# Banded attention into a squared-ReLU feed-forward network: weight loads, column writes, PSUM pools and zeroing rearranged in the first third of the kernel

## The chip, the cores and the metric

One core of a Trainium2 chip runs the whole program. The metric is the device time of one execution in microseconds (us), lower is better; a version is given as the median of several executions. The engines are named as in the profile: PE multiplies matrices (PEld is its weight load, which overlaps), DVE is the vector engine, ACT the scalar engine, POOL the GpSimd engine, and SP only starts transfers. Each engine works through its own instructions in program order and waits where an input is not ready. Transfers (DMA) are started from SP, ACT and POOL; the ones from POOL can change the number type on the way, and here they turn float32 in memory into float16 on chip.

## What is computed

Eight batches of eight heads, 576 tokens of 64 numbers each. Every token attends to tokens within 32 positions; eight "global" tokens, whose positions are an input, attend to all and are attended by all. The result goes through a two-layer network.

```python
scores = (1 / sqrt(64)) * q @ k.T                      # per batch and head, 576 x 576
mask = |pos_i - pos_j| <= 32  or  i is global  or  j is global
attn = softmax(where(mask, scores, -1e9))
x = (attn @ v)  as 4608 tokens x 512                    # heads side by side
h = x @ w_in                                            # 512 x 2048
out = (relu(h) ** 2) @ w_out                            # 2048 x 512
```

The eight positions are known only when the kernel runs, so the kernel cannot place them at build time.

## The kernel before, in words

**Layout.** Work is done by pair of heads: `i = 4*b + hp` is pair `hp` of batch `b`, so pairs 0 to 3 are batch 0 and pairs 4 to 7 batch 1. A pair's keys lie in five tiles of 128 rows (8 rows for the global tokens, then 120 tokens), its queries in 608 columns (four groups of 144 tokens and 8 columns for the global tokens). Each pair is done in two halves: `sc_mm` (L766) makes the scores, `sc_exp` (L786) the exponentials on ACT, `sc_mask` (L794) the mask on DVE, `pv_mm` (L811) the products with the values and the sums, `pv_rec` (L829) the reciprocal of the sums on ACT as exp(-ln), `pv_mul` (L859) the division on DVE into `xT` (for the first half of batch 0 into `xA`), the transposed input of the network. The global tokens' own results are summed over column groups in `pv_sum` (L835), divided into `gx`, and written into their columns of `xT` or `xA` by `scatter` (L881): eight small copies on POOL, one for each global token, whose column comes from a register. In batch 0 `pv_sum` finishes pairs 0 to 2 in one go (at `hp` = 2) and pair 3 alone.

**Network.** `mm1_half` and `mm1` are the first product with ReLU and square; `mm2` is the second product of chunk 0, `mm2_fast` (L686) that of the later chunks, as seven half-sized products in place of eight, which need sums of weight blocks (`weight_sum`, L632, five of them, on DVE, into the `early` buffer that holds batch 0's and 1's values before) and sums of activation blocks. This work stands in a list, `fills`. `fill(n)` (L745) takes pieces from its head for `n` units of credit, with fixed costs per kind (L748), as long as the tokens they need are done (`done[0]`). So network work is laid between the steps of attention at build time, in an order that each engine then follows.

**Batch 0, written out by hand (L899 to L1027).** Queries, keys and values come by transfers from SP and ACT for pairs 0 and 1 (L218 to L224) and from POOL for pairs 2 and 3 (L291 to L295). DVE zeroes some areas first (`stv[0:NG]` L231, `vts[2]` and `vts[3]` L233), POOL four others (L290). POOL then starts, in this order: the four slices of `w_in` (L979), the tokens of batch 1 (L986 to L989), register loads of the positions and `scatter` of pairs 0 to 2 (L991), two slices of `w_out` (L1005), `scatter` of pair 3 (L1006), the other two slices (L1012), and `scatter` of the second halves (L1013). SP holds the values of batch 1 back behind a small transfer `gate` (L1015) that waits for the third slice of `w_in`.

**PSUM.** Matrix products land in PSUM, in tiles by tag: `at` (two banks each, attention) and `mm` (one bank each). All lie in one pool: three `at` and two `mm` at first; after the last scores of batch 0, `open_psum(2, 4)` (L998) closes the pool and opens another with two `at` and four `mm`. A pool opened after another takes its place in PSUM, so its first use waits until the old pool's tiles are read.

After that switch, PE does 24 matrix products of `mm1_half` (four tiles `u` = 0, 2, 4, 6, three of four pairs: L1000), `pv(2, 1)` and `pv(3, 1)`, eight more products for pair 3 (L1008), and goes on with the fills and batch 1.

**Batch 1 to 2.** At the end of batch 1 comes `fill(3)` (L1060), then for batch 2 onward, per pair: both halves of scores, `weight_sum` calls while `b == 2` (two at pair 0, two at pair 1, one at pair 2; L1073), `fill(4)`, the products with the values, and `fill(4)` again (L1090).

Of the kernel before, what the change touches and what calls it, by code (L numbers as in the profile page):

```python
# [18 lines left out]
NT = 5  # L19
# [31 lines left out]
def kernel(  # L51
# [10 lines left out]
    nc = tc.nc  # L62
# [4 lines left out]
    P = 128  # L67
# [17 lines left out]
    psum = {}  # L85

    def open_psum(at, mm):
        if psum:
            psum["stack"].close()
        psum["stack"] = ExitStack()  # L90
        psum["pool"] = psum["stack"].enter_context(
            tc.tile_pool(name=f"ps{at}", bufs=1, space=bass.MemoryType.PSUM)
        )
        psum["bufs"] = {"at": at, "mm": mm}

    def pst(tag, shape, dtype=FP32):
        return psum["pool"].tile(shape, dtype, name=tag, tag=tag, bufs=psum["bufs"][tag])

    open_psum(3, 2)
# [131 lines left out]
    nc.vector.memset(stv[0:NG, :, 0 : 2 * 2], 0.0)  # L231
    for vt in vts[2:NHP]:
        nc.vector.memset(vt[0:NG], 0.0)  # L233
# [55 lines left out]
    for vt in vts[0:NHP]:  # L289
        nc.gpsimd.memset(vt[96:P, 4], 0.0)  # L290
# [3 lines left out]
    for i in range(2, NHP):  # L294
        fetch_values(nc.gpsimd, 0, i, vts[i])  # L295
# [431 lines left out]
    W1, W2 = 0.65, 1.54  # L727
# [17 lines left out]
    def fill(n):  # L745
        credit[0] += n
        while fills and fills[0][0] <= done[0]:
            cost = {mm1: W1, mm2_fast: W2}.get(fills[0][1], 1) * share[0]  # L748
            if credit[0] < cost / 2:
                break  # L750
            credit[0] -= cost
            take(1)
        else:
            credit[0] = min(credit[0], 0)

    share = [1.0]

# [77 lines left out]
    def pv_sum(i, half):  # L835
# [10 lines left out]
        if (half == 0 and b == 0 and hp >= NHP - 2) or (half and b and hp == NHP - 1):  # L846
            gs = gsum[b][:, 0]
            a, z = (0, NHP) if b else (0, NHP - 1) if hp < NHP - 1 else (NHP - 1, NHP)
            if b:
                nc.vector.tensor_tensor(out=gs, in0=gs, in1=gsum[b][:, 1], op=ALU.add)  # L850
            gr = sbt("gr", [P, NHP, NG], FP32, bufs=2)
            if a == 0:
                gxs[b] = sbt("gx", [P, NHP, NG], FP16, bufs=2)
            nc.vector.reciprocal(out=gr[:, a:z], in_=gs[:, a:z, 1])
            nc.vector.tensor_tensor(
                out=gxs[b][:, a:z], in0=gs[:, a:z, 0], in1=gr[:, a:z], op=ALU.mult
            )
# [28 lines left out]

    wv = moe_w_in.rearrange("(t p) f -> p t f", p=P)
    wo = moe_w_out.rearrange("(t p) m -> p t m", p=P)
# [89 lines left out]
    for i in range(4):  # L978
        pool.dma_start(out=w_in[:, :, ts(i, 512)], in_=wv[:, :, ts(i, 512)])  # L979
# [5 lines left out]

    for nm in "kq":  # L986
        fetch_tokens(pool, nm, NHP)
    for nm in "kq":
        fetch_tokens(pool, nm, NHP + 1, NHP - 1)  # L989
    load_columns()  # L990
    scatter(0, slice(0, NHP - 1), xA)  # L991
# [6 lines left out]
    open_psum(2, 4)  # L998
    wide[0] = True
    for u in range(0, 8, 2):  # L1000
        mm1_half(u, 0, range(NDM - 1))
    pv(2, 1)
    pv(3, 1)
    for j in range(2):
        pool.dma_start(out=w_out[:, ts(j, 4), :], in_=wo[:, ts(j, 4), :])  # L1005
    scatter(0, slice(NHP - 1, NHP), xA)  # L1006
    nc.scalar.copy(out=xT[:, :, 256:HS], in_=xA[:, :, 256:HS])
    for u in range(0, 8, 2):  # L1008
        fills.pop(0)
        mm1_half(u, 0, range(NDM - 1, NDM))  # L1010
    for j in range(2, 4):
        pool.dma_start(out=w_out[:, ts(j, 4), :], in_=wo[:, ts(j, 4), :])  # L1012
# [47 lines left out]
    fill(3)  # L1060
    wide[0] = False

    for i in range(2 * NHP, B * NHP):
# [9 lines left out]
        if b == 2:  # L1073
            for p in ((3, 4), (6, 7), (1,), ())[hp]:
                weight_sum(p)
            if hp == 0:
                nc.gpsimd.memset(vbs[1][96:P, NT - 1], 0.0)
        fill(4)
# [11 lines left out]
        fill(4)  # L1090
# [9 lines left out]
    psum["stack"].close()  # L1100
# [30 lines left out]
```

## Time and profile before

| | us |
|---|---|
| median of 4 executions (327.37 to 331.79) | 330.08 |
| the profiled execution, whole | 331.15 |
| its span, first to last instruction of the program | 329.4 |

The four times spread over 4.4 us. The profile belongs to one execution, whose span is 1.75 us shorter than its own whole time. Five views are read. The page gives busy time per engine and the span in 40 slices of 8.2 us. The windows view gives, for chosen stretches, busy time and count of instructions per engine, and the clock that was granted to PE (1.00 is full speed). The timeline lists instructions in order: start, duration, engine, line, operation, what is written and read, count, and in brackets how long the engine stood idle before and what ended that. The view of waits adds such idle times up. The view of transfers gives their queues and rates. "Issue" in a bracket means that no wait is visible in the profile.

Instructions of PE are pipelined and a busy PE can be one that works at half speed, so the clock column has to be read beside the busy column.

### The profile page before, as it was taken

To read this page: it belongs to the slowest core of one execution; us is meant where nothing else is said; L and a number is where in the kernel's file an instruction comes from. 1 tells how busy PE (TensorE), PEld (TensorE's weight loads), DVE (VectorE), ACT (ScalarE), POOL (GpSimd) and SP (SyncE) were. 2 spreads that over 40 slices of the span, in tenths; PEclk is the share of its full clock that TensorE was granted. 3 is DMA by queue.
4 is the path that set the end of the run, shared out by engine and by line. 5 is a ranking of instruction groups with operands and counts; after the bars stand their busy time and mean duration, and the time that the engine had idled before them with its cause. 6 is when DMAs were issued, how large, how long until landed. Compare 5 with 4: busy or idle time off the path is not lost.

```text
span 329.4 us, 11606 instructions
## 1 busy us (share of the span) xinstructions
PE 312.3 (95%) x4827; PEld 237.2 (72%) x4827; DVE 244.5 (74%) x595; ACT 200.9 (61%) x378; POOL 127.6 (39%) x222
## 2 busy tenths in 40 slices
PE   6977899999989999999999999999999999999995
PEld 3655678545569857975799865985698569868995
DVE  7756278849799778876967969876987698758465
ACT  2567458745767587667457478658865876363150
POOL 8945389318910880089200773039402000100000
PEclk9995799999999999999999999999999999999999
DMA  8999999939991999299924299959995400200211
GB/s 191 145 201 199 200 195 160 150 76 107 196 148 39 149 187 148 53 146 167 159 76 109 30 164 150 73 131 173 134 86 129 123 4 16 87 30 2 68 63 66
DMA packets 149492, 38.98 MB, mean 118 GB/s; under 512 B 132696, under 2 KB 148872, under 8 KB 149440
## 3 DMA queue, kind: packets, MB, share of 16 engines
q0 software_dynamic: 97872, 17.08, 66.5%
q1 hardware_dynamic: 51150, 20.57, 31.5%
q8 instruction: 38, 0.62, 0.9%
q10 hardware_dynamic: 418, 0.59, 0.7%
q14 instruction: 14, 0.11, 0.1%
HBM read 37.80 MB, written 17.29 MB: 167 GB/s over the span
## 4 chain that ended last, share of the span: by engine, by line
issue 42%; POOL 20%; PE 17%; DMA 6%; DVE 3%; ACT 1%; POOLq 1%
PE mm L305 16%; POOL kscr L183 6%; DMA qscr<-in_q_dram 6%; POOL xT L884 4%; POOL stf L212 3%; POOL qscr L190 2%; POOL s16b L212 2%; DVE gt L556 1%; POOL gstk L442 1%; DVE mix L641 1%; POOL gstq L442 1%; POOL gstv L442 1%; POOLq L884 1%; PE at L822 1%; ACT er L790 1%
## 5 line engine op out<-in xcount | busy, mean ns | idle before, releaser
L305 PE MATMUL mm<-xT,w_in 128*64 128x512 f16 (+2 forms) x1216 | 122.5, 351 | 0.2 <-POOL xT L884 0.2
L305 PEld LDWEIGHTS <-w_in 128*64 128x64 f16 (+1 forms) x1280 | 80.5, 110 | 46.0 <-issue 3.4
L554 ACT ACTIVATE rl<-mm 128x512 f16<-128x512 f32 x128 | 74.3, 600 | 36.7 <-PE mm L305 33.6
L884 POOL COPY xT<-gx 128x4 f16 x64 | 17.7, 277 | 141.0 <-DVE xT L863 137.6
L556 DVE TENSOR_TENSOR gt<-rl 128x512 f16<-128x512 f16 x128 | 52.9, 421 | 24.3 <-ACT rl L554 20.7
L305 PEld LDWEIGHTS <-mix 128*64 128x64 f16 x1280 | 68.9, 110 | 1.6
L790 ACT ACTIVATE er<-at 128x880 f16<-128x880 f32 x58 | 49.7, 904 | 15.4 <-PE at L781 13.9
L641 DVE TENSOR_TENSOR mix<-gt 128x1024 f16<-128x1024 f16 (+1 forms) x82 | 52.8, 670 | 0.2
L800 DVE TENSOR_TENSOR et<-er,mask 128x880 f16<-128x880 f16 x58 | 35.7, 616 | 17.9 <-ACT er L790 17.3
L305 PE MATMUL mm<-early,mix 128*64 128x256 f16 x768 | 45.4, 273 | 0.0
L832 ACT ACTIVATE rec<-at 128x288 f32<-128x288 f32 x64 | 25.9, 404 | 29.3 <-PE at L822 23.0
L305 PEld LDWEIGHTS <-gt 128*64 128x64 f16 (+1 forms) x596 | 33.1, 109 | 11.1 <-DVE gt L556 3.5
L863 DVE TENSOR_TENSOR xT<-at,rec 128x288 f16<-128x288 f32 x60 | 27.1, 452 | 10.5 <-ACT rec L833 9.9
L305 PE MATMUL mm<-early,gt 128*64 128x256 f16 x512 | 32.2, 274 | 2.3 <-DVE gt L556 2.3
L822 PE MATMUL at<-et,onesb 128*64 128x192 f16 (+5 forms) x400 | 31.1, 230 | 0.0
L305 PE MATMUL mm<-w_out,mix 128*64 128x256 f16 x512 | 30.9, 273 | 0.0
L833 ACT ACTIVATE rec<-rec 128x288 f32<-128x288 f32 x64 | 28.4, 443 | 2.0
L676 DVE TENSOR_TENSOR ot<-mm,pt 128x512 f32<-128x512 f32 (+1 forms) x36 | 22.7, 631 | 6.5 <-ACT pt L701 5.2
L183 POOL DMA_DIRECT2D kscr<-in_k_dram x30 | 26.3, 1083 | 0.3 <-issue 0.3
L190 POOL DMA_DIRECT2D qscr<-in_q_dram x24 | 24.5, 1526 | 0.0
L822 PEld LDWEIGHTS <-onesb 128*64 128x64 f16 x400 | 22.8, 114 | 0.7
L701 ACT COPY pt<-mm 128x512 f32<-128x512 f32 (+1 forms) x18 | 9.7, 540 | 20.5 <-PE mm L305 20.5
(125 smaller groups left out, 325.8 us busy)
## 6 DMA issues: line engine op xcount, KB each, us to landing
out_dram<-ot SPq DMA_DIRECT2D x32, 256.0 KB
qscr<-in_q_dram POOLq DMA_DIRECT2D x24, 144.0 KB
kscr<-in_k_dram POOLq DMA_DIRECT2D x24, 120.0 KB
w_in<-in_moe_w_in_dram POOLq DMA_DIRECT2D x4, 512.0 KB
w_out<-in_moe_w_out_dram POOLq DMA_DIRECT2D x4, 512.0 KB
early<-in_v_dram SPq DMA_DIRECT2D x12, 120.0 KB
stf<-in_v_dram POOLq DMA_DIRECT2D x12, 120.0 KB
s16b<-in_v_dram POOLq DMA_DIRECT2D x12, 120.0 KB
```

Of the source, the lines that this page charges most:

```text
L183: nc.gpsimd.dma_start(out=kscr[b][r0 : r0 + KN[t]].rearrange("s (h d) -> s h d", d=D), in_=k[b, :, KT * t : KT * t + KN[t]].rearrange("h s ...
L190: nc.gpsimd.dma_start(out=qscr[b][r0 : r0 + GTOK].rearrange("s (h d) -> s h d", d=D), in_=q[b, :, GTOK * g : GTOK * (g + 1)].rearrange("h ...
L305: nc.tensor.matmul(to[r], weights[:, r], moving, **flags)
L554: nc.scalar.activation(out=rl, in_=ph, func=AF.Relu)
L556: nc.vector.tensor_tensor(out=gt[:, :, 0:T], in0=rl, in1=rl, op=ALU.mult)
L641: nc.vector.tensor_tensor(out=gsums[p][:, lo:hi, 0:TH], in0=g[0], in1=g[1], op=op)
L790: nc.scalar.activation(out=er[:, :, 0:W], in_=scs.pop((i, half))[:, :, 0:W], func=AF.Exp, bias=0.0, scale=scale)
L800: nc.vector.tensor_tensor(out=et[:, :, 0:W], in0=er[:, :, 0:W], in1=mask[:, MB[half] : MB[half] + W].unsqueeze(1).to_broadcast((P, 2, W)), ...
L822: nc.tensor.matmul(acc[D * e : D * e + D, x, o : o + w], onesb if x else vt[:, t, e], et[:, e, so : so + w], start=(n == 0), stop=(n == le ...
L833: nc.scalar.activation(out=rec, in_=rec, func=AF.Exp, scale=-1.0)
L863: nc.vector.tensor_tensor(out=(xT if x0 else xA)[:, hp, x0 : x0 + HS].rearrange("p (k x) -> p k x", k=2), in0=av[:, 0, :, 0:GTOK], in1=rec ...
L884: nc.gpsimd.tensor_copy(out=xb[:, :, ds(gv[g], 1)], in_=gxs[b][:, pairs, g : g + 1])
```

## The change

It has five parts.

1. Zeroing: `stv[0:NG]`, `vts[2]` and `vts[3]` are zeroed by copies of a zero tile on ACT; rows 96 on of the fifth tile of `vts[2]` and `vts[3]` too; the same rows of `vts[0]` and `vts[1]` by DVE. POOL zeroes none of them.
2. POOL's transfers: the first slice of `w_in` is started between the values of pairs 2 and 3, the second after those of pair 3, the other two where all four were.
3. Column writes of batch 0: `pv_sum` finishes pairs 0 and 1 together and pairs 2 and 3 together. `scatter` of pairs 0 and 1 goes ahead of the transfers of batch 1's tokens on POOL, `scatter` of pairs 2 and 3 behind them; all `w_out` slices come after both. `mm1_half` runs in two parts of two pairs (16 and 16 products, where it was 24 and 8).
4. PSUM: the third `at` buffer lies in a pool of its own. Only that pool is closed at the switch, and its two banks become two more `mm` buffers; the two `at` and two `mm` of the base pool stay. `pst` counts its calls and sends each third `at` tile (before the switch), or each second `mm` tile (after it), to the extra pool, so the buffers take turns as they did.
5. Batch 2: five times `fill(1.6)` with one `weight_sum` each before the loop, in place of `fill(3)` and the `weight_sum` calls in the loop; `done[0]` is 2 before it; inside batch 2 each `fill(4)` becomes `fill(slot)`, an 8.5th of what is left.

```diff
-    def open_psum(at, mm):
-        if psum:
-            psum["stack"].close()
...
+    psum_base = open_psum("base", {"at": 2, "mm": 2})
+    psum_more = open_psum("third", {"at_more": 1})
 
     def pst(tag, shape, dtype=FP32):
-        return psum["pool"].tile(shape, dtype, name=tag, tag=tag, bufs=psum["bufs"][tag])
-
-    open_psum(3, 2)
+        n = banks_of[tag]
+        banks_of[tag] += 1
+        more = tag + "_more"
+        if more in pools and (n % 3 == 0 if tag == "at" else n % 2):
+            tag = more
+        pool, bufs = pools[tag]
+        return pool.tile(shape, dtype, name=tag, tag=tag, bufs=bufs)
...
-    nc.vector.memset(stv[0:NG, :, 0 : 2 * 2], 0.0)
+    zeros = idle[0:NG].unsqueeze(1)[:, :, 0 : 4 * D].to_broadcast((NG, NT, 4 * D))
+    nc.scalar.copy(out=stv[0:NG, :, 0:4].rearrange("p t h d -> p t (h d)"), in_=zeros)
     for vt in vts[2:NHP]:
-        nc.vector.memset(vt[0:NG], 0.0)
+        nc.scalar.copy(
+            out=vt[0:NG].rearrange("p t e d -> p t (e d)"), in_=zeros[:, :, 0 : 2 * D]
+        )
+        nc.scalar.copy(out=vt[96:P, 4].rearrange("p e d -> p (e d)"), in_=idle[96:P, 0 : 2 * D])
+    for vt in vts[0:2]:
+        nc.vector.memset(vt[96:P, 4], 0.0)
...
-    for vt in vts[0:NHP]:
-        nc.gpsimd.memset(vt[96:P, 4], 0.0)
+    def fetch_w_in(i):
+        nc.gpsimd.dma_start(out=w_in[:, :, ts(i, 512)], in_=wv[:, :, ts(i, 512)])
...
-    for i in range(2, NHP):
-        fetch_values(nc.gpsimd, 0, i, vts[i])
+    fetch_values(nc.gpsimd, 0, 2, vts[2])
+    fetch_w_in(0)
+    fetch_values(nc.gpsimd, 0, 3, vts[3])
+    fetch_w_in(1)
...
-        if (half == 0 and b == 0 and hp >= NHP - 2) or (half and b and hp == NHP - 1):
+        if (half == 0 and b == 0 and hp % 2) or (half and b and hp == NHP - 1):
             gs = gsum[b][:, 0]
-            a, z = (0, NHP) if b else (0, NHP - 1) if hp < NHP - 1 else (NHP - 1, NHP)
+            a, z = (0, NHP) if b else (hp - 1, hp + 1)
...
-    for i in range(4):
-        pool.dma_start(out=w_in[:, :, ts(i, 512)], in_=wv[:, :, ts(i, 512)])
+    for i in range(2, 4):
+        fetch_w_in(i)
...
+    load_columns()
+    scatter(0, slice(0, 2), xA)
     for nm in "kq":
         fetch_tokens(pool, nm, NHP)
     for nm in "kq":
         fetch_tokens(pool, nm, NHP + 1, NHP - 1)
-    load_columns()
-    scatter(0, slice(0, NHP - 1), xA)
+    scatter(0, slice(2, NHP), xA)
...
-    open_psum(2, 4)
+    pools.pop("at_more")
+    psum_more.close()
+    psum_more = open_psum("fourth", {"mm_more": 2})
     wide[0] = True
     for u in range(0, 8, 2):
-        mm1_half(u, 0, range(NDM - 1))
+        mm1_half(u, 0, range(2))
     pv(2, 1)
     pv(3, 1)
     for j in range(2):
-        pool.dma_start(out=w_out[:, ts(j, 4), :], in_=wo[:, ts(j, 4), :])
-    scatter(0, slice(NHP - 1, NHP), xA)
+        fetch_w_out(j)
     nc.scalar.copy(out=xT[:, :, 256:HS], in_=xA[:, :, 256:HS])
     for u in range(0, 8, 2):
         fills.pop(0)
-        mm1_half(u, 0, range(NDM - 1, NDM))
+        mm1_half(u, 0, range(2, NDM))
...
-    fill(3)
+    done[0] = 2
+    for p in (3, 4, 6, 7, 1):
+        fill(1.6)
+        weight_sum(p)
     wide[0] = False
+    slot = left() / 8.5
...
-        if b == 2:
-            for p in ((3, 4), (6, 7), (1,), ())[hp]:
-                weight_sum(p)
-            if hp == 0:
-                nc.gpsimd.memset(vbs[1][96:P, NT - 1], 0.0)
-        fill(4)
+        if i == 2 * NHP:
+            nc.gpsimd.memset(vbs[1][96:P, NT - 1], 0.0)
+        fill(slot if b == 2 else 4)
```

## The prediction, made before the changed kernel was run

> **What bounds the kernel now.** I read the windows view first, cut at stages, since the page's busy shares average over stages with different limits.
>
> ```profile
> core 0: us, PE busy (x) PEld busy (x) DVE busy (x) ACT busy (x) POOL busy (x), PEclk, DMA share, GB/s
> 0.00:10.07 10.07, 6.79 (x76) 3.97 (x78) 7.13 (x46) 3.20 (x7) 8.79 (x31) 1.00 0.92 195
> 10.07:23.72 13.65, 11.13 (x295) 8.29 (x291) 8.94 (x25) 8.14 (x21) 9.40 (x13) 1.00 1.26 165
> 23.72:37.37 13.65, 11.72 (x119) 8.17 (x115) 5.46 (x17) 6.73 (x12) 6.48 (x20) 0.50 1.28 202
> 37.37:48.00 10.63, 8.88 (x164) 7.21 (x160) 7.17 (x21) 7.21 (x16) 6.59 (x13) 1.00 1.19 191
> 48.00:72.00 24.00, 23.80 (x346) 15.19 (x342) 17.96 (x51) 16.68 (x34) 12.48 (x14) 1.00 1.63 145
> 72.00:112.00 40.00, 38.87 (x576) 27.31 (x576) 33.13 (x70) 25.40 (x47) 21.48 (x37) 1.00 1.11 119
> 112.00:280.00 168.00, 165.85 (x2578) 127.25 (x2576) 133.11 (x304) 115.35 (x212) 60.80 (x89) 1.00 1.08 114
> ```
>
> From 48 us on PE is busy 97% to 99% of each stage: it is the limit there, and a microsecond won earlier arrives at the end undiminished if transfers keep up. Room lies before 48 us: PE is idle 9.5 us of it (48 minus 38.5), and from 23.72 to 37.37 us it has half its clock. There the timeline shows what PE, DVE, ACT and POOL do:
>
> ```profile
> 1.63 1.12 DVE L231 MEMSET early<- 8x1280 f32 x1 [0.22 <-issue]
> 2.77 0.66 DVE L233 MEMSET early<- 8x320 uint32 x2
> 6.34 0.83 ACT L462 CAST natq<-stf 96x768 f16<-96x768 f32 x1 [4.24 <-DMA stf<-in_q_dram]
> 22.76 0.24 PE L478 MATMUL mm<-early,oh 128*64 128x128 f16 x1 [1.71 <-issue]
> 27.62 2.02 POOL L884 COPY mix<-gx 128x3 f16 x8 [7.84 <-DVE mix L863]
> 31.28 2.33 POOL L884 COPY mix<-gx 128x1 f16 x8
> 31.77 5.28 PE L305 MATMUL mm<-mix,w_in 128*128 128x256 f16 x24 [1.42 <-ACT er L790]
> 37.81 0.41 ACT L832 ACTIVATE rec<-at 128x288 f32<-128x288 f32 x1 [6.14 <-issue]
> 40.21 1.91 PE L305 MATMUL mm<-mix,w_in 128*128 128x256 f16 x16 [1.13 <-ACT rl L587]
> ```
>
> The reader sees: DVE zeroes for 1.8 us while ACT stands idle for 4.2; PE waits 1.42 us at the PSUM switch for an exponential; 24 products then take 5.28 us, 220 ns each at half clock (the later 16 take 119 ns each), and ACT sits 6.14 us behind them, because `pv(2, 1)` comes after all 24. PE then waits again, 1.13 us, for the ReLU that frees a PSUM buffer.
>
> **The change part by part.** All against the profiled execution, 331.15 us whole, 1.07 us over the median of 330.08.
>
> *Zeroing.* DVE loses 1.12 + 0.66 us and gains two memsets of the kind at L1030 (0.11 us each): 1.55 us sooner at the mask and at the cast of pair 0's keys (6.82 us, their transfer landed at 4.1). PE follows as far as queries allow: their cast waits for a landing at 6.34 us whatever is done, so their transposes go from 8.39 to about 7.2 us. I take 1.1 us for what comes after. The copies on ACT are not in this trace; its nearest row, the cast above, is 0.83 us for 768 elements, so 1280, twice 640 and twice 128 cost about 3.3 us behind the table load's end at 2.1 us and two issues: they end near 5.6 us, before 6.34. Without that cover, each excess microsecond would delay the query cast. Bounds for this part: 0 (a later chain hides it) to 1.5. POOL loses 0.7 us of memsets, which starts its transfers as much sooner.
>
> *Weight slices.* POOL's queue gets `w_in` 0 and 1 ahead of where they stand (0.78 us of issue each). Behind slice 0 wait the three issues of pair 3's values, which landed at 15.8 us; a slice took about 3 us in the steady stretch (19.9, 23.1, 25.6, 28.6 us), so they land near 17 to 18. PE reads them at 23.75. The gather of global values moves past both slices, landing near 20 in place of 16.5; only SP's store waits for it. The transfers have a hole at 14 to 16 us (58 and 38 GB/s by microsecond, about 200 around it), which the early slices fill, so slice 3 lands 2 to 3 us sooner and the gate opens sooner. PE needs slices 0 and 1 only at about 29 us: the direct gain is nothing, and so is the cost, with 5 us of cover over pair 3's values.
>
> *Column groups.* On POOL the first scatter becomes pairs 0 and 1; its input is `pv_mul(1, 0)`, done at 25.7 us (24.6 after the gain above), so it runs to about 26.7. Behind it now stand four token transfers (2.95 us of issue, formerly at 17.0 to 19.8), then scatter 2 to about 32 us (eight copies again, 2.0 to 2.3 us). No queue entry is cheaper: 16 copies before, 16 after. Tokens of pair 4 then land near 31 us, and those of the others, 0.86 MB at the 150 KB/us that POOL's queue gets beside SP's, near 36. They are used at 42.0 and 46.4 us, some 4 us sooner after the change: covered by 5 us. The four `w_out` slices go behind, as before first read after 50 us.
>
> *PSUM and the order on PE.* The first `mm` tile is in the base pool and free; the new one waits only for `pv_mul(1, 1)`, at 30.6 us. So the 1.42 us go. In place of 24 products ahead of `pv(2, 1)` there are 16. With the cold clock of this profile: scores of pair 3 end at 30.35 - 1.1 = 29.25; 16 x 220 ns = 3.5, to 32.8; the two `pv_mm` 1.4, to 34.2; the other 16 products at 119 ns, 1.9, to 36.1 (their scatter ended at about 32). ACT begins its reciprocals at about 33.5, takes 1.7 for both, 0.3 for the copy and 0.6 for the first ReLU: 36.2. PE goes on there in place of 40.21: 4.0 us sooner, 1.1 of it from zeroing, 2.9 from this part. What is late next is POOL's second scatter.
>
> If PE were at full clock throughout, the before would be some 3.6 us shorter here (24 x 0.1 us at the products, the rest from 119 smaller matmuls that stretch, an estimate), the new order would stop at POOL's second scatter (31.2 us) and PE would resume near 33.3, so about 3.3 us stay.
>
> *Batch 2.* The five `weight_sum` take 1.22 us each on DVE. Three of them lie in a stage where DVE is the limit:
>
> ```profile
> 72.00:80.00 8.00, 8.00 (x94) 4.29 (x94) 5.77 (x10) 3.31 (x7) 6.65 (x15) 1.00 0.70 45
> 88.00:96.00 8.00, 7.64 (x102) 4.46 (x98) 8.00 (x20) 6.70 (x14) 3.60 (x5) 1.00 2.01 145
> 96.00:104.00 8.00, 7.43 (x148) 7.10 (x150) 8.00 (x17) 4.05 (x8) 0.00 (x0) 1.00 0.49 57
> ```
>
> DVE works without a pause from 88 to 104 us, and PE is idle 0.93 us of it, mostly behind squares (`gt`, L556) queued on DVE. The change moves the sums to about 72 to 80 us, where DVE has 2.2 us free and the eight remaining `mm2` pieces (about 0.9 us each, 7 us) keep PE busy without it. Counting the credits through the list, the 8 units before the loop are exactly those eight pieces; the first scores of batch 2 move behind five more of them, 4.5 us later against the network work, none of which is lost. Their masks queue behind the last sum, and six `mm1` pieces (5.4 us) cover that on PE. Pieces of chunk 1 need `scatter(1)`, done at 74.6 us, before PE gets there at 78. In the later batches the same pieces stand in the same slots but for one. Bounds: -0.5 (masks late at the start of batch 2) to 1.6 (the idle PE of 88 to 112 us, less what other stages have too). I take 1.0.
>
> *A rule against the row.* PE stands idle for 1.7 us until 22.76 us, with no wait visible, and 1 us later the clock falls to half for 13.65 us. The Trainium skill ("TensorE: Matmul & The Clock Gate", sections "What's actually happening" and "Why this matters for your kernels") has half clock follow a whole idle window of about 3.4 us, and warns of idle gaps over about 3 us. By that rule this gap is too short, the cold stretch is no property of this order of work, and the changed kernel should not be charged with one: it would come back at 33.3 us instead of 36.2, 2.9 us more gain. By the row, 1.7 us in the midst of thin work were enough. The instructions around the gap are unchanged, so I keep the gap and the fall, and take the row's value; the rule's is the lower end of the range. (13.65 us are four times 3.41 us; the length of the window the trace bears out.)
>
> **Sum.** 1.1 + 2.9 + 1.0 = 5.0 us: 326.15 us for an execution like the profiled one. The four times (327.4 to 331.8) spread by about what the cold stretch is worth, so the median is likely of executions with less of it; there the gain is 3.3 to 4.0 plus 1.0, giving 325.1 to 325.8 from 330.08. I forecast 325.8.
>
> **The rivals.**
> *Cold stretch gone or shorter.* PE gets dense work 2.5 us sooner, which can end the half clock one window sooner, or the gap falls otherwise in the window. For: the clock came back just after the 24 products. Against: the gap stays. Time: 326.15 - 2.9 = 323.3.
> *The gain is partly hidden.* Zeroing gains nothing because the chain through ACT and the landing at 6.34 us sets the start, or moving the sums only shifts DVE's queue. For: queries cannot be cast sooner. Against: DVE and PE have no idle time worth the name between 5 and 7 us. Time: 330.08 minus only 2.2 to 2.9, some 327.2 to 327.9; with the PSUM wait left besides (see next), 329.3.
> *The change does not do what it says.* If the new pool's first tile waits for all scores as the old one did, the 1.42 us stay: 327.2. The first tile is in the pool that is never closed, which speaks against it.
> *Slower: POOL's second scatter stalls PE.* Scatter copies took 0.25 us each in these groups but 0.40 beside a busy DVE (3.17 us for eight at 40.1). Twice 3.2 and the tokens' 2.95 from 24.6 us end at 34.0 instead of 32; any further 2 us (a late `pv_mul(1, 0)`, slower issues while queues are full) let PE stand 1.8 us or more between its two sets of 16 products. By the row above that is a gap that halves the clock, and PE's next 13.65 us, about 70% matmul time, would cost 5 us. It decides where the scatter ends later than 36 us in a cold execution, or 33 in a warm one; without the clock it costs only its own length. Time: 330.08 - 4.3 + 2.8 + 5.0 = 333.6.
>
> **How the numbers follow.** Likeliest case (324.3 to 327.2): 0.48. Cold stretch gone (322.3 to 324.3): 0.16. Partly hidden or not as said (327.2 to 331): 0.25. POOL stall (331 to 336): 0.11. The range from 322.8 to 330.3 leaves out about 0.05 below and 0.13 above. One per cent, 3.3 us, is about what a measurement of this kernel can tell from no change; faster than that means below 326.8. Of the likeliest case 0.40 lies there, with 0.16 of the cold one: 0.56. Slower than 333.4: 0.07. The rest, 0.37, is within 1%.
>
> **What the profile would show.** Right: the cast of pair 0's keys near 5.3 us and scores of pair 3 over a microsecond sooner; 16 products at the switch with no idle time before them; no 6 us gap on ACT; network work after the switch resuming near 36 us or sooner, not 40.2; DVE below 8 of 8 us somewhere in the stage that was 88 to 104; stages after 112 us of the same length. Wrong: PE idle before the second 16 products with POOL's scatter as the releaser; the transposes of batch 1's tokens (42.0 us before) starting after a transfer's landing; a second stretch at half clock; PE idle before the first `mm1` of chunk 1 behind DVE. If the stages from 48 us on lengthen by what the start gains, the claim that PE alone sets them was wrong.

## The result and the profile after

| | us | of it |
|---|---|---|
| before, in the same comparison | 328.09 | median of 65 executions, 326.72 to 332.20 |
| after | 327.18 | median of 42 executions, 324.75 to 330.09 |
| ratio after to before | 0.9957 | 95% interval 0.9941 to 0.9973 |
| profiled execution, after | 325.63 | span 323.9 |

The change gains 0.9 us, 0.43%: more than the comparison's uncertainty, and well within 1%. The forecast was 325.8 from a base of 330.08, a gain of 4.3. Two of these numbers have to be explained: the median of before lies 2 us below that of the four times that were shown, and the gain is a fifth of what was summed. The gain of more than 1%, to which the forecast gave 0.56, did not come.

The profile alone tells another story. The windows view, cut from the start of full clock at 7.56 us in steps of 13.65 us, with one later stage:

```profile
core 0: us, PE busy (x) PEld busy (x) DVE busy (x) ACT busy (x) POOL busy (x), PEclk, DMA share, GB/s
0.00:7.56 7.56, 5.75 (x55) 3.10 (x57) 4.95 (x40) 5.66 (x11) 6.34 (x25) 1.00 0.80 192
7.56:21.21 13.65, 11.49 (x308) 8.37 (x305) 9.40 (x29) 8.22 (x22) 9.29 (x11) 1.00 1.43 199
21.21:34.87 13.66, 10.70 (x167) 8.35 (x162) 8.20 (x23) 10.62 (x23) 9.82 (x26) 1.00 0.95 143
112.00:280.00 168.00, 165.05 (x2628) 128.26 (x2625) 133.74 (x303) 113.53 (x209) 57.88 (x92) 1.00 1.06 111
```

The stretch at half clock is not there. The timeline of the start, with line numbers of the changed kernel (L910 is the scatter's copy, L889 the product of `pv_mul`, L858 and L859 the two steps of the reciprocal):

```profile
5.55 0.55 DVE L485 CAST natk<-stf 96x768 f16<-96x768 f32 x1
20.94 0.24 PE L501 MATMUL mm<-early,oh 128*64 128x128 f16 x1 [1.11 <-issue]
23.81 0.26 PE L848 MATMUL at_more<-et,early 128*64 128x160 f16 x2 [1.40 <-ACT rec L859]
23.82 1.98 POOL L910 COPY mix<-gx 128x2 f16 x8 [6.59 <-DVE mix L889]
28.38 0.60 PE L328 MATMUL mm_more<-mix,w_in 128*128 128x256 f16 x4 [0.38 <-DVE xT L889]
28.71 2.60 POOL L910 COPY mix<-gx 128x2 f16 x8
30.84 0.41 ACT L858 ACTIVATE rec<-at 128x288 f32<-128x288 f32 x1 [1.50 <-PE at L848]
31.36 0.60 PE L328 MATMUL mm_more<-mix,w_in 128*128 128x256 f16 x4 [0.19 <-POOL mix L910]
33.23 1.03 PE L328 MATMUL mm_more<-mix,w_in 128*128 128x256 f16 x8
56.36 1.04 PE L328 MATMUL mm_more<-w_out,gt 128*128 128x512 f16 x4 [0.67 <-DVE qt L559]
```

The keys are cast 1.27 us sooner (5.55 for 6.82), and the wait of 1.42 us at the PSUM switch is 0.38 us. The gap of 6.14 us on ACT is 1.50 us. The second part of `mm1_half` starts at 31.36 us (before, its eight products stand at 38.03), and the work that stood at 40.21 starts at 33.23. But two new waits stand in the list. Pair 2's first values wait 1.40 us for the one buffer of `at_more`, where the profile of before shows 0.35 us at that place. The buffers do not take turns as they did: here these values have to wait until pair 1's values are divided (L889 on DVE, which ended at 23.76 us, in the same instant as the reciprocal that the row names). And in batch 1 an output tile waits 0.67 us for a buffer that pair 7's queries hold. Scores of pair 4 start 6.98 us sooner (38.11 for 45.09), and the span ends 5.52 us sooner. So a pair of profiles shows six times what the medians show.

### The profile page after: what moved, and what is told of

Read it like the earlier page. It is cut to its first block, busy times and chain, and to the rows that moved or that the text cites. A ratio compares the mean times of both kernels' runs of the same rounds, so it can differ in the third digit from the quotient of the medians.

```text
span 323.9 us, 11561 instructions
## 1 busy us (share of the span) xinstructions
PE 307.0 (95%) x4807; PEld 232.7 (72%) x4807; DVE 245.6 (76%) x594; ACT 203.7 (63%) x383; POOL 133.0 (41%) x218
## 4 chain that ended last, share of the span: by engine, by line
PE 50%; issue 24%; POOL 9%; DVE 7%; ACT 3%; DMA 2%; POOLq 2%; DVEq 0%; ACTq 0%
PE mm_more L328 23%; PE mm L328 20%; PE at L848 4%; PE at L807 2%; DMA qscr<-in_q_dram 2%; DVE gt L579 2%; DVE mix L664 2%; POOL xT L910 2%; ACT er L816 1%; POOL kscr L191 1%; POOL mix L910 1%; POOLq L905 1%; DVE et L826 1%; ACT rl L577 1%; POOL early L170 1%
## 5 line engine op out<-in xcount | busy, mean ns | idle before, releaser
L328 PEld LDWEIGHTS <-w_in 128*64 128x64 f16 (+1 forms) x1280 | 78.7, 109 | 43.0 <-issue 1.1
L910 POOL COPY xT<-gx 128x4 f16 x64 | 20.8, 326 | 124.8 <-DVE xT L889 121.4
L328 PE MATMUL mm_more<-xT,w_in 128*64 128x512 f16 (+2 forms) x608 | 70.9, 352 | 0.2 <-POOL xT L910 0.2
L328 PE MATMUL mm<-xT,w_in 128*64 128x512 f16 (+2 forms) x608 | 70.8, 351 | 0.0
L577 ACT ACTIVATE rl<-mm_more 128x512 f16<-128x512 f32 x64 | 38.2, 598 | 20.0 <-PE mm_more L328 19.8
L577 ACT ACTIVATE rl<-mm 128x512 f16<-128x512 f32 x64 | 38.5, 602 | 13.3 <-PE mm L328 10.1
L858 ACT ACTIVATE rec<-at 128x288 f32<-128x288 f32 x60 | 24.2, 403 | 27.2 <-PE at L848 27.2
L889 DVE TENSOR_TENSOR xT<-at,rec 128x288 f16<-128x288 f32 x59 | 26.8, 454 | 8.1 <-ACT rec L859 7.4
L328 PE MATMUL mm_more<-early,mix 128*64 128x256 f16 x512 | 31.1, 273 | 0.0
L859 ACT ACTIVATE rec<-rec 128x288 f32<-128x288 f32 x64 | 28.4, 443 | 2.0
L848 PE MATMUL at<-et,onesb 128*64 128x192 f16 (+3 forms) x364 | 27.1, 227 | 0.0
L807 PE MATMUL at<-qt,kt 64*128 64x192 f16 (+5 forms) x400 | 19.8, 223 | 2.0 <-DVE xT L889 1.4
L807 PEld LDWEIGHTS <-kt 64*128 64x128 f16 x400 | 12.1, 94 | 13.3 <-issue 11.9
```

Of the source, the lines that this page charges most:

```text
L328: nc.tensor.matmul(to[r], weights[:, r], moving, **flags)
L577: nc.scalar.activation(out=rl, in_=ph, func=AF.Relu)
L807: nc.tensor.matmul(sc[:, e, so : so + w], kt[r, t, :], qt[r, c0 : c0 + w], start=not added(i, half), stop=True, skip_group_check=True,)
L848: nc.tensor.matmul(acc[D * e : D * e + D, x, o : o + w], onesb if x else vt[:, t, e], et[:, e, so : so + w], start=(n == 0), stop=(n == le ...
L859: nc.scalar.activation(out=rec, in_=rec, func=AF.Exp, scale=-1.0)
L889: nc.vector.tensor_tensor(out=(xT if x0 else xA)[:, hp, x0 : x0 + HS].rearrange("p (k x) -> p k x", k=2), in0=av[:, 0, :, 0:GTOK], in1=rec ...
```

## Experiments

Each kernel was timed against before on the chip of its set. The first four ran on one chip (before there: 327.81 us), the next four on a second (327.66), the last four on a third (325.78). Absolute times are therefore compared within a set, and ratios across sets.

### The changed kernel again, and three parts undone

`after_again` is the changed kernel unedited. `undo_zero` restores the three memsets on VectorE and the four on GpSimd. `undo_batch2` restores the place of the weight sums and the fill of batch 2. `one_pool` restores the single pools that are closed and opened at the switch and keeps the rest:

```
-    pools.pop("at_more")
-    psum_more.close()
-    psum_more = open_psum("fourth", {"mm_more": 2})
+    open_psum(2, 4)
```

`after_again`: 

> The changed kernel once more, for a second profile: the first profiled execution (325.63 us) was 1.55 us faster than the median of the changed kernel (327.18), and the profiled execution of before 3.06 slower than its median (328.09), so the pair of profiles shows 5.5 us where the medians show 0.9. Theory A (the typical execution loses its extra 1.5 us at the change from batch 1 to batch 2, where the column writes on POOL took 4.89 us beside the weight sums on DVE, 0.5 us short of stalling PE): PE idle at the first first-layer product of chunk 1 with POOL as releaser, about 1.5 us. Theory B (it is lost before 40 us, by a stretch of half clock or by an idle PE): scores of pair 4 begin 1.5 us later than 38.1 us, the later stages are as long as in the first profile. Median 326.7 to 327.7.

`undo_zero`: 

> The changed kernel with the zeroing on DVE and POOL as before. If the 1.3 us that the first scores gained in the profiles are real and carried to the end: 1.1 us slower than the changed kernel, about 328.3. If a later chain hides them (the column writes on POOL, or the random state of the clock): within 0.4 us, 327.2.

`undo_batch2`: 

> The changed kernel with its fifth part undone: fill(3) before batch 2, weight sums inside batch 2, fill(4). Theory A: the column writes of batch 1 run beside nothing on DVE and take about 2 us again; 1 to 1.5 us faster than the changed kernel, about 325.9. Theory B: this part has little to do with it; the same to 1 us slower, 327.2 to 328.2 (the prediction's 1.0 us for the part).

`one_pool`: 

> The changed kernel with PSUM as before: one pool, closed and opened again with two and four buffers. Theory of the prediction: PE waits at the switch for the exponentials of pair 3, about 1.3 us, but in batch 1 the wait of 0.67 us of the extra pool (a second-layer product waiting for the query transposes of pair 7, since it may only take one of two buffers) goes: 0.6 us slower, 327.8. Rival (the split costs more than the wait it removes, in batch 1 and later): 0.5 to 1 us faster, 326.4.

| kernel | median us | ratio to before, 95% | profiled us | scores of pair 0 / pair 4 start |
|---|---|---|---|---|
| after_again | 326.73 | 0.9959 (0.9932 to 0.9986) | 327.27 | 9.99 / 40.16 |
| undo_zero | 326.71 | 0.9965 (0.9940 to 0.9990) | 327.48 | 10.80 / 39.07 |
| undo_batch2 | 326.79 | 0.9979 (0.9956 to 1.0001) | 327.12 | 10.12 / 38.85 |
| one_pool | 328.04 | 0.9999 (0.9972 to 1.0025) | 327.93 | 9.96 / 39.42 |

Only `one_pool` loses the gain: its median lies 1.3 us above that of `after_again` on the same chip, though the intervals of the two ratios still overlap. So the split of the pools carries the gain. But its waits do not add up to it. The timeline of `one_pool`:

```profile
23.84 0.26 PE L840 MATMUL at<-et,early 128*64 128x160 f16 x2 [0.63 <-ACT et L808]
29.64 1.91 PE L320 MATMUL mm<-mix,w_in 128*128 128x256 f16 x16 [1.43 <-ACT er L808]
```

The wait at the switch is 1.43 us here and 0.38 in both profiles of the changed kernel, so 1.05 us are won. Pair 2's values wait 0.63 us here and 1.40 there, so 0.77 us are lost: with one pool they start when the exponential of pair 3's scores has ended (23.79 us), 0.7 us before pair 1's division ends (24.55). The 0.67 us of the output tile are lost too. By these three waits the split would cost 0.4 us. What makes up the 1.3 us of the medians is not shown by them; a clock that is halved less often is one candidate (see below).

The zeroing moves pair 0 by 0.8 us and the median by nothing. The second profile of the changed kernel shows what can hide it: its transposes were at half clock until about 16.3 us, those of the first until 7.56. That differs from execution to execution of the same kernel, is worth 2 us at pair 4 (40.16 against 38.11, so theory B held), and a gain of 1 us ahead of it is lost in it. The ten products of pair 0's first scores took 0.40 us, as at full clock, in all five profiles with the old zeroing, and 0.58 us in four of the nine with the new one. Whether the new zeroing brings these late starts is not settled by so few.

`undo_batch2` has the median of `after_again` (326.79 and 326.73 us) and waits in batch 2. Its timeline at the first scores of batch 2:

```profile
68.95 0.56 PE L807 MATMUL at<-qt,kt 64*128 64x160 f16 x12 [1.09 <-DMA qt<-qscr]
```

The transposing transfers of pair 8 can be late when PE comes sooner. The five pieces that the change puts ahead of those scores cover this wait, which is all that part is seen to do. It has a price on GpSimd, seen in two timelines, first of before and then of after: the scatter of batch 1 takes 4.89 us where it lies beside the sums, and 2.05 us where it did not (2.04 in `undo_batch2`).

```profile
72.56 2.05 POOL L884 COPY xT<-gx 128x4 f16 x8 [12.08 <-DVE xT L863]
```

```profile
66.39 4.89 POOL L910 COPY xT<-gx 128x4 f16 x8 [4.70 <-DVE xT L889]
```

It ends at 71.28 and PE reads it at 71.84, so nothing is lost yet.

### Was the profile of before typical?

`before_again`: 

> The kernel before, unchanged. If the execution that the forecast read was an unusually cold one (its 13.65 us at half clock), another profiled execution shows at most one stretch of 3.4 us at half clock behind the start, the scores of pair 4 begin near 41 to 42.5 us instead of 45.09, the median is again near 328 us and the ratio 1.000 within 0.003. If the forecast's base was typical, pair 4 begins near 45 us again, with more than 8 us at half clock between 20 and 40 us, and the median is near 330.

Measured: 328.35 us, ratio 1.0013 (0.9982 to 1.0043). The profiled execution took 328.03 us, and pair 4 starts at 41.47. Its windows view:

```profile
22.57:25.99 3.42, 2.40 (x57) 1.78 (x56) 2.64 (x9) 3.36 (x7) 0.16 (x1) 1.00 1.25 212
25.99:29.40 3.41, 1.46 (x27) 1.03 (x27) 2.31 (x7) 3.00 (x6) 2.84 (x10) 1.00 1.28 202
29.40:32.81 3.41, 3.41 (x19) 2.43 (x17) 0.30 (x1) 0.00 (x0) 2.86 (x11) 0.50 1.31 188
32.81:36.22 3.41, 2.65 (x39) 2.04 (x38) 0.79 (x2) 1.96 (x6) 0.29 (x1) 1.00 1.25 195
```

and its timeline:

```profile
21.40 0.24 PE L478 MATMUL mm<-early,oh 128*64 128x128 f16 x1 [0.39 <-issue]
23.50 0.26 PE L822 MATMUL at<-et,early 128*64 128x160 f16 x2 [0.63 <-ACT et L790]
29.15 4.45 PE L305 MATMUL mm<-mix,w_in 128*128 128x256 f16 x24 [1.49 <-ACT er L790]
```

One stretch of 3.41 us at half clock, not four. The forecast read an execution 3.6 us more delayed at pair 4 than this one. Against this profile, `after` is 3.36 us sooner at pair 4 and 2.40 us at the end of the span. The wait at the switch is there in both (1.49 and 1.42 us), so it belongs to the kernel; the cold stretch of 13.65 us belonged to the execution.

The windows also show what stood ahead of the half clock. The reader is to look at PE's busy time in the row ahead of a 0.50: here 1.46 of 3.41 us, 43%. In the profile of before the row ahead was 20.30 to 23.72 us:

```profile
20.30:23.72 3.42, 1.71 (x43) 1.18 (x37) 1.24 (x4) 1.30 (x4) 0.00 (x0) 1.00 1.24 204
23.72:27.13 3.41, 3.06 (x43) 1.97 (x37) 2.40 (x10) 2.53 (x5) 0.00 (x0) 0.50 1.25 209
```

which is 50%.

### Groups, an earlier full clock, and the third tile

`undo_groups` restores the sums after pairs 3 and 4 of batch 0, one scatter of three pairs and one of the last, and three row tiles ahead of the values. `warm_first` adds one warming product at the start (a product of zeros that nothing reads). The other two edits:

```
# warm_first
-    keep_warm(4)
+    keep_warm(5)
     index_base()
# third_tile, in mm2
         if part == 0:
+            banks_of["mm"] += m == 2
             po_now[m] = pst("mm", [P, 512])
+            banks_of["mm"] += m == 3
```

`undo_groups`: 

> The changed kernel with the old groups of global columns: sums after the third and fourth pair, one scatter of three pairs behind the token fetches and one of the last pair behind the first two slices of the second weight, and three of the four row tiles multiplied before the second halves of pairs 2 and 3 instead of two. If the groups are covered, as the forecast has it (cost nought), the median stays within 0.5 us of 326.7. If they carry part of the gain, TensorE waits at the fourth row tile for the last pair's columns, over 0.5 us with the copies of GpSimd named, and the median is 327.3 or more. If the second scatter beside the token fetches is what costs in the changed kernel, undoing it is faster: 326.2 or less.

Measured: 327.62 us, ratio 0.9977 (0.9945 to 1.0010). The median lies in the expected loss, but no copy of GpSimd is named at the fourth row tile (the wait there, 1.07 us, is for a ReLU), and the interval holds the changed kernel's 0.9957. Whether the median loses is undecided. The wait for a ReLU itself belongs to the old groups: it is 1.13 us in before, 1.07 here and 1.07 in `pool_alone` below, and is not there in the changed kernel.

`warm_first`: 

> The changed kernel with five instead of four warming products before the indices, which fills TensorE's idle 0.55 us from 3.18 to 3.73 us. If the start of full clock is what differs between executions (7.6 us in one profile of the changed kernel, about 16 us in the other), an uninterrupted start lets the first whole busy stretch of 3.4 us end between 4.7 and 8.1 us instead of between 7.1 and 10.6 us: scores of pair 0 begin near 9.0 us each time, and at about 0.35 us lost for each us at half clock the median falls by 0.5 to 0.9 us, to 325.8 to 326.2. If the start is bound by the loads and VectorE instead, pair 0 begins where it did and the median stays within 0.3 us of 326.7.

Measured: 327.30 us, ratio 0.9964 (0.9929 to 0.9999). Pair 0 starts at 8.74 us as expected, and full clock is there at 6.19. The median does not fall: in 5 of its 12 executions the mean clock is below 0.988. The profile fell on such a one:

```profile
19.84:23.25 3.41, 1.58 (x24) 1.03 (x24) 1.56 (x7) 1.36 (x3) 0.00 (x0) 1.00 1.24 206
23.25:26.67 3.42, 2.47 (x34) 1.53 (x36) 1.91 (x6) 1.78 (x6) 1.85 (x9) 0.50 0.58 100
26.67:30.08 3.41, 2.88 (x45) 2.22 (x44) 1.49 (x6) 3.20 (x6) 3.12 (x8) 0.50 0.77 137
30.08:33.49 3.41, 3.41 (x16) 2.15 (x16) 1.24 (x2) 0.93 (x2) 3.17 (x8) 0.50 1.14 172
33.49:36.90 3.41, 3.21 (x45) 2.65 (x45) 1.26 (x3) 2.66 (x8) 1.53 (x4) 1.00 1.27 192
```

This is the changed kernel, but for one warming product, with 10.24 us at half clock. The cold stretch can still come back; it came after a row with PE busy 46%, which holds a gap of 1.60 us, put down by the profile to the transfer of the gathered values, and part of the new wait for `at_more`. Pair 4 starts at 41.45 here, 3.3 us later than in the profile of after.

`third_tile`: 

> The changed kernel with the third output tile of the first chunk taken from the base pool instead of the pool of the fourth bank. If the 0.67 us wait in batch 1 is the split's own (the third tile may only use the buffer that pair 7's queries hold), it is gone, with 0.2 us or less in its place, and batch 1's last scores begin 0.6 to 0.7 us sooner against those of pair 4; if what follows covers nothing the median falls to 326.0 to 326.2. If the key transposes or the relu of the same pair end last instead, the wait stays over 0.4 us under another name, and the median stays at 326.7.

Measured: 326.57 us, ratio 0.9951 (0.9912 to 0.9989). The wait is gone. The timeline of its output tiles, the third line being the third tile:

```profile
51.72 1.04 PE L328 MATMUL mm_more<-w_out,gt 128*128 128x512 f16 x4
54.05 1.04 PE L328 MATMUL mm<-w_out,gt 128*128 128x512 f16 x4
55.83 1.04 PE L328 MATMUL mm<-w_out,gt 128*128 128x512 f16 x4
```

Pair 7's second scores start 22.05 us behind pair 4's first, 22.82 in after: 0.77 us won, and the ratio is not told apart from 0.9957. Within the uncertainty of these medians 0.7 us can't be seen.

### Bridging the idle time; slices; the split alone

`before_bridge` and `third_bridge` put warming products into a free bank where PE is idle. `third_bridge` has the edit of `third_tile` too, and its `bridge` does not count the tile that it takes:

```
+    def bridge(n):
+        warm(pst("mm", [P, 512]), n)
+        banks_of["mm"] -= 1  # only in third_bridge
...
     pv_mul(1, 0)
+    bridge(3)            # 5 in third_bridge
     pv_mm(2, 0)
...
-    pv_mm(1, 1)
+    pv_mm(1, 1, 2)
     sc_mm(2, 1)
+    bridge(2)
     sc_mm(3, 1)
+    bridge(6)            # 1 in third_bridge
```

`before_bridge`: 

> The kernel before with 13 warming products (as the start's, into a free bank) put where TensorE stands idle between 20 and 29 us: three before pair 2's first values, two before pair 1's second values, two before pair 3's second scores, six before the split of the banks. Nothing of the change is in it. If the clock is halved when a stretch of 3.41 us was busy for half of it or less (50, 43 and 46 per cent in the three profiles where it was halved, 54 or more where it was not), no stretch there is below 60 per cent any more, no half clock follows, and the median falls from about 327.7 to about 326.6, the median of the executions of before that ran at full clock: a ratio of 0.996 to 0.997, as large as the change's own. If the change's gain is the removed wait of 1.42 us itself, warming products bring nothing: 327.5 or more.

`third_bridge`: 

> The changed kernel with the third output tile in the base pool and ten warming products in its idle stretches between 20 and 29 us (five before pair 2's first values, two before pair 1's second, two before pair 3's second scores, one before the split). If what is left between executions of the changed kernel is the half clock, its median falls to that of the executions at full clock, 325.9 to 326.1, no execution lies above 328, and the ratio is 0.993 to 0.995. If the spread comes from the loads instead, the median stays at 326.6 to 327.2 with executions above 328.

`undo_slices`: 

> The changed kernel with the first two slices of the first weight back behind the values, at the place of the other two. If they are worth nought, as the forecast has it, the median is within 0.5 us of the changed kernel's 326.7 to 327.2. If they keep the weight ahead of the tokens, undoing it makes the first products of that weight wait for a transfer, named by DMA, by 0.5 us or more, and the median is 327.5 or more.

`pool_alone`: 

> The kernel before with the split of the banks' pools alone (no zeroing, slices, groups or sums of the change). If the split removes the wait before the first products of the network (1.42 us in the profile of before, 1.49 us in the second) and with it the stretch that halves the clock, half clock becomes rarer and the median falls to 326.7 to 327.2. If the gain needs the regrouped columns and the sums as well, since the time is only passed on to the transposes of pair 8, the median stays at 327.5 to 328, though scores of pair 4 begin near 40 us.

| kernel | median us | ratio to before, 95% | at full clock |
|---|---|---|---|
| before, third chip | 325.78 (29 executions) | 1 | 2 of 29 |
| before_bridge | 325.48 (12) | 0.9989 (0.9968 to 1.0009) | 10 of 12 |
| pool_alone | 324.96 (12) | 0.9979 (0.9952 to 1.0007) | 10 of 12 |
| undo_slices | 326.22 (12) | 1.0009 (0.9982 to 1.0036) | 2 of 12 |
| third_bridge | 323.11 (6) | 0.9910 (0.9875 to 0.9945) | 4 of 6 |

"At full clock" counts executions whose mean granted clock is 0.9985 or more. The others are a mixture, since a stretch after PE's last work lowers the mean too. One stretch of 3.41 us in 325 takes 0.005 off the mean, so an execution at 0.996 or more has none such ahead of that; counted this way it is 7 of 29 for before, 11 of 12 for `before_bridge` and 10 of 12 for `pool_alone`.

The bridge does to the clock what was expected of it. In the windows view of `before_bridge` no row between 22 and 32 us is below 90%:

```profile
22.00:25.42 3.42, 3.42 (x64) 2.16 (x61) 2.55 (x8) 2.83 (x7) 0.00 (x0) 1.00 1.24 207
25.42:28.83 3.41, 3.17 (x58) 1.87 (x54) 1.97 (x8) 3.19 (x7) 2.16 (x9) 1.00 1.27 204
28.83:32.24 3.41, 3.15 (x30) 2.33 (x27) 1.24 (x2) 0.77 (x1) 2.86 (x11) 1.00 1.33 197
```

But the time it wins is not what was expected: 0.3 us and not told apart from none, where 1.0 or more was forecast. On this chip the two executions of before at full clock have 325.02 (the seven at 0.996 or more 324.96), so only about 0.8 us were to be had. Full clock in `before_bridge` has a median of 325.35, so some 0.3 us went elsewhere. The profile shows one such place, at the first scores of batch 2:

```profile
69.03 0.56 PE L784 MATMUL at<-qt,kt 64*128 64x160 f16 x12 [1.14 <-DMA qt<-qscr]
```

It is the wait of `undo_batch2` again: what is won at the start is in part waited for at pair 8. (`pool_alone` came there at 67.78 us without a wait, so the time at which PE comes is not all that sets it.) So this run does not rule the clock out as the source of the change's gain.

`pool_alone` gains 0.8 us, with an interval that just holds nothing, and has its clock at full in 10 of 12 executions. With `one_pool` (everything but the split: nothing gained) this points at the split from both sides. But 0.8 us are also what before loses here by its clock: its seven executions at 0.996 or more have a median of 324.96, the ten of `pool_alone` 324.76. So on this chip the split's gain goes with fuller clock, and little is seen beside it. Its own price shows in its timeline, the wait of pair 2's values:

```profile
24.39 0.26 PE L830 MATMUL at_more<-et,early 128*64 128x160 f16 x2 [1.25 <-DVE mix L871]
28.96 0.81 PE L313 MATMUL mm_more<-mix,w_in 128*128 128x256 f16 x6 [0.44 <-DVE xT L871]
```

`undo_slices` went against the forecast: its ratio lies above the changed kernel's 0.9957, and the intervals (from 0.9982 up, and up to 0.9973) don't touch. No transfer is named by a wait of PE in its profile, so the expected mechanism is not shown either; the profiled execution had half clock from 25.80 to 36.04 us behind a row with PE busy 1.47 of 3.42 us. The changed kernel did not run on that chip. Whether the early slices are worth half a per cent, and by which way, stays open.

`third_bridge` lies 2.7 us under before on the same chip, more than expected, with no execution above 324.95. In its timeline 1.24 us of warming products stand where the wait for `at_more` was:

```profile
21.97 1.24 PE L328 MATMUL mm<-idle 128*64 128x512 f16 x9
23.53 0.26 PE L854 MATMUL at_more<-et,early 128*64 128x160 f16 x2 [0.32 <-DVE mix L895]
```

Its profile fell on the slowest of the six executions, so where the 1.8 us beyond the change's own 0.9 come from is not seen. Its interval reaches the changed kernel's, and the two were not timed side by side.

## Why the prediction was right and wrong

**The base.** The prediction's sum was 5.0 us from the profiled execution, and the forecast a gain of 4.3 from 330.08, the median of four executions. That median is 2.0 to 2.4 us above the three of before from the first comparisons (328.09, 327.81, 327.66). The sum was also made against one of the coldest executions: of the 122 executions of before in the first two sets (`before_again` included), 11 had a mean clock below 0.988, and the profiled one, with 13.65 of 329.4 us at half clock, has 0.979. That the number 325.8 lies 1.4 us from the measured 327.18 is luck: two errors partly cancel, a base 2 us too high and a gain 3.4 us too large.

**The term that failed most: PSUM and the order on PE, 2.9 us.** Its mechanism is mostly there as forecast: 16 products of 109 ns stand at the switch, the gap on ACT is 1.50 us, and the wait of 1.13 us is gone. Of the 1.42 us, 0.38 are left, because the first products took a tile of the new pool (`mm_more`) and not, as the forecast had it, the free one of the base pool. The size was taken from the cold execution, and it missed what the split costs. The third slot is now one buffer with fixed users, so pair 2's values wait 1.40 us for pair 1's (0.63 us in `before_again` and in `one_pool`), and the third output tile waits 0.67 us. `pool_alone` measured 0.8 us (with an interval that holds nothing) and `one_pool` 1.3 us (326.73 against 328.04) for the split. How much of that is the wait at the switch and how much a clock that is halved less often was not separated. The prediction asked only whether the first tile of the new pool was free, not who else is bound to one buffer.

**Cold stretch.** The forecast kept it because the row had a gap of 1.7 us at the right place, though the rule that it quoted asks for a longer one. The length of the gap does not decide it: gaps of 1.43 and 1.49 us at that place (`third_tile`, `undo_groups`) brought no fall, one of 1.17 us (`undo_slices`) did, and none was as long as 3 us. Once full clock had begun and before 38 us, half clock followed in all the profiles when PE's busy time in one row of 3.41 us was 50, 43, 46 or 43%; the lowest shares after which it did not follow were 54, 56, 56 and 58%. These four stretches ended with the first row that was busy throughout.

The busy share is not the whole of it, though. At the end of the kernel a row of 41% kept full clock through the next one, in which PE did nothing. In `after_again`:

```profile
320.09:323.50 3.41, 1.40 (x26) 1.13 (x22) 1.69 (x4) 0.00 (x0) 0.00 (x0) 1.00 0.42 145
323.50:326.92 3.42, 0.00 (x0) 0.00 (x0) 0.00 (x0) 0.00 (x0) 0.00 (x0) 1.00 0.02 5
```

And at the start a row that was busy throughout did not end the half clock in `undo_slices`: it was busy 3.42 us from 8.73 to 12.15, but the next products of `values_sum`, three of them at 12.63, still took 0.48 us, where they took 0.33 us in `after` at full clock.

Whether a kernel meets a row that is half idle depends on where the rows fall in an execution. Full clock began at 7.56 and about 16.3 us in two profiles of the same kernel; counted back in steps of 3.41 us, the rows begin at 0.7 us in one and at 2.6 in the other. The Trainium skill ("TensorE: Matmul & The Clock Gate", section "What's actually happening") calls that window free-running, which these starts bear out, but the idle window that it asks for was not needed here: one that was half idle was enough. So the rival "cold stretch gone" came true, for about half of the executions: 34 of 66 of the changed kernel ran at full clock (0.9985 or more), 21 of 122 of before (first two sets, and the result's own executions for the changed kernel). It did not bring 323.3, because before without it is 326.55 and the changed kernel without it 326.10. At equal clock these medians leave 0.45 us of the change, over several chips; on the one chip that is known to have run both, 0.18 (or 0.68, with the line at 0.996). None of these is clear of the spread. So fewer cold executions may be half of the gain or more, which no run shows by itself.

**Zeroing, 1.1 us.** The cast comes 1.27 us sooner and pair 0's scores 1.58. In the medians nothing: 326.71 without it, 326.73 with it. The rival named ACT's chain as the cover, but the copies on ACT ended at 5.53 us, as forecast, ahead of the queries at 6.34. What can cover it is the start of full clock. Besides, 18 of 22 executions ran at full clock without the new zeroing (median 326.71) and 10 of 22 with it (326.19): a gain at equal clock may be paid for with colder executions, which so few do not show.

**Slices and groups, nought.** The cover of the tokens held: no transposes of batch 1 started late in a profile of after. Undoing the slices cost half a per cent by its ratio, undoing the groups an undecided 0.2% or none; that both are worth nothing is not confirmed. The rival of a stall on GpSimd did not come: the second scatter cost PE 0.19 us.

**Batch 2, 1.0 us.** VectorE is relieved as said. The windows view of after:

```profile
88.00:96.00 8.00, 7.76 (x160) 7.33 (x162) 7.08 (x18) 5.37 (x11) 1.38 (x2) 1.00 1.91 152
96.00:104.00 8.00, 7.81 (x156) 7.05 (x154) 5.79 (x13) 4.35 (x8) 1.06 (x6) 1.00 0.47 117
```

VectorE is busy 7.08 and 5.79 us of 8, and PE 0.5 us more than before in these 16, though the work in them is further on by the earlier start. From 112 to 280 us PE stands idle 2.95 us instead of 2.15, but 2.33 in `after_again`, so most of that loss is the execution's. By the medians the part is worth 0.06 us, and it covers a wait that an earlier start can make.

**Claim that time won before 48 us arrives at the end undiminished.** It mostly does when two executions are compared (3.36 us at pair 4 and 2.40 at the end, `after` against `before_again`; the output tile's 0.67 us lie between). What failed is that an execution's start is a draw: pair 4 began between 38.11 and 41.45 us in executions with the changed kernel's order.

## What to carry to other kernels

Before summing gains against a profile, ask which part of it is the kernel's and which the execution's: compare its own time with the spread of all times, and take a second profile where the clock changed. Where a split gives a tile pool fixed users for each buffer, ask of every user, not only of the first, who held that buffer last. Look for a risk of half clock in PE's busy share over a stretch of some 3.4 us and not only in its longest gap; idle time that can't be removed can be filled with products into a free bank, and what those cost has to be measured too.

## What the runs showed of the hardware

- Once full clock had begun and before 38 us, rows of 3.41 us with PE busy 50% and less were followed by half clock (four profiles), rows of 54% and more were not (ten profiles). At the end of the kernel rows of 41% (`after_again`) and 43% (`before_bridge`) were not followed by it and one of 32% (`third_tile`) was, so the share alone does not set it.
- The same instruction of PE, the third product of `values_sum(2)`, stood for 1.71, 0.39, 1.11, 0.39, 1.49 and 1.43 us without a visible wait in `before`, `before_again`, `after`, `after_again`, `undo_groups` and `third_tile`. The kernel's order does not set that length; its cause was not tried.
- Eight copies of GpSimd took 2.05 us in before, 2.04 in `undo_batch2`, and 4.89 us beside the weight sums of VectorE.
- Chips differ by more than this change: before has medians of 327.66 to 328.09 us in three comparisons and 325.78 us on the last chip.
